# Gated linear attention and a two-level mixture of experts: token pairs of two sequences on the partitions

## The chip, the cores and the metric

One Trainium2 chip, one core. The metric is the device time of the whole kernel in microseconds (us); a run's time is that of the slowest core, and here there is one. TensorE is called PE, its weight loads PEld, VectorE DVE, ScalarE ACT, GpSimd POOL, SyncE SP.

## The reference, cut to what matters

Inputs q, k, v, f_logit have the shape (4 sequences, 8 heads, 768 tokens, 48), in float32.

```
f = sigmoid(f_logit)
for t in range(768):                                   # for each sequence and head
    state = f[t, :, None] * state + outer(k[t], v[t])  # 48 x 48
    y[t]  = q[t] @ state
x = y, heads side by side                              # (3072 tokens, 384)
g = argmax(x @ w_group);  e = argmax(x @ w_expert[g])  # 4 groups of 4 experts
out[token] = softmax weight of g * softmax weight of e * relu(x @ w1[g, e]) @ w2[g, e]
```

The expert matrices are 384 x 1024 and 1024 x 384; each token goes through one of 16 experts.

## The kernel before, in words

**Two stages.** The first computes the attention and the routing, the second sends the tokens of each expert through its two matrices ("passes"). Two early passes, on experts chosen from the first four chunks of tokens, fill PE at the seam of the two stages.

**The attention** is done in chunks of 128 tokens. A unit is one chunk of two sequences with their 8 heads; there are 12 units, two to a chunk (`units`). Tokens lie on the 128 partitions, and for each of the two sequences (index `b`) the free side holds 8 heads of 48 numbers. The work of a unit is cut into steps, each a generator, named by letters in `STAGES`:

- `l` (`load`): four transfers from SP's queue, of f, k, q and v, 384 KB each, in runs of 48 numbers (192 bytes).
- `c` (`bounded`): DVE clamps f from below (L581). `g` (`gated`): ACT makes -log f with Exp and Ln (L591, L594); PE sums it over the tokens up to each token by a product with the triangle `tri` (L600, tile cs, one for each sequence); ACT exponentiates cs with both signs into eq and kh (L601, L602); POOL issues the transfer of the last token's row into `ends` (L607).
- `m` (`multiplied`): DVE makes qh = q*eq and kh = k*min(kh, bound) (L620, L623).
- `t` (`turned`): PE transposes qh and kh, head pairs together (L634), ACT copies them out as Tq and Tk (L635). `b` (`decayed`): the chunk's decay factors, from `ends` (L644, copied out at L645).
- `s` (`scored`): PE multiplies Tk by Tq into the scores ap (L660), in products of 48 x 64 (weights) by 128 columns on quarters of the array; DVE masks them with `tri` into am (L663).
- `n` (`stated`): PE sums kh by v into ds (L677), 16 products with 128 tokens as rows, 64 weight columns, 48 moving columns; DVE adds the old state and multiplies by the decay (L683, L684).
- `w` (`weighed`): PE adds old state by Tq (L698) and v by am (L702, 16 products with 128 rows and 64 weight columns) into y; ACT copies y into xT (L705).
- `d` (`done`): PE makes the logits from xT (lT L718, lg L723), DVE adds them up (L724). `x` (`listed`): PE transposes xT to rows (L743), ACT copies them (L745, L748). `r`: one step of the routing (`route`), which is a chain of some 24 small DVE operations for a chunk, three small groups of PE products (rk L203 and L205, tb L251), and on POOL the issue of a transfer of `meta` (L246).

**The order of the work** on PE, DVE, ACT and SP is written out by hand: the lists `BEGIN` (the first units), `EVEN`, `ODD` and `ORDERS` (the last units) say for each unit i which step of which neighbour comes next (`d-2` is the next step of `d` for unit i-2), and these engines run in that order. POOL's order is chosen by the scheduler when the program is built. An EVEN and an ODD iteration together carry two units and one chunk's routing.

**PSUM** has 8 banks; `bank` hands them out in rotation, so that an allocation waits until the one eight before it has been read.

**The second stage**, 18 passes with the early ones: `up` (hp, L439), `down` (yo, L475 and L460), gathers and scatters of rows by POOL's indirect transfers (L393, L450). The change does not touch it but for the order in which `bank` hands out banks.

Of the kernel before, what the change touches and what calls it, by code (L numbers as in the profile page):

```python
# [18 lines left out]
P = 128  # L19
# [4 lines left out]
def kernel(  # L24
# [42 lines left out]
    ps = ctx.enter_context(tc.tile_pool(name="ps", bufs=8, space=bass.MemoryType.PSUM))  # L67
# [12 lines left out]
    def bank(shape, name):  # L80
        return ps.tile(shape, FP32, tag="bank", name=name)
# [12 lines left out]
    halves = const([P, 2], FP32, "halves")  # L94
    make_upper_triangular(nc, tri, val=1.0, diag=True)
    make_identity(nc, ident)
    nc.vector.memset(onesb, 1.0)
    nc.vector.tensor_tensor(strictb, tri, ident, OP.subtract)

# [419 lines left out]
    with ExitStack() as fast:  # L519
# [7 lines left out]
        for nm, count in (("v", 4), ("eq", 2), ("qh", 3), ("kh", 3)):  # L527
            pads[nm] = [kept([P, 2, H, DP], f"{nm}{i}") for i in range(count)]
        states = [[kept([P, 2, HP, DP], f"st{s}_{i}") for i in range(2)] for s in range(B // 2)]

        def padded():

            for n in range(4):
                for nm in ("eq", "qh", "kh", "v"):
                    if n < len(pads[nm]):
                        nc.vector.memset(pads[nm][n][:, :, :, D:DP], 1.0 if nm == "eq" else 0.0)
                if n == 1:
                    for t in sum(states, []):
                        nc.vector.memset(t[:, :, :, D:DP], 0.0)
                    nc.vector.memset(gw, 0.0)  # L540
                if n < 3:
                    yield
            constants()
            yield
# [9 lines left out]
        def heads(t):  # L554
            return t.rearrange("p b h d -> p (b h) d")

# [5 lines left out]
        SRC = {"f": f_logit, "k": k, "qh": q, "v": v}  # L562

        def parts(i):

            return (slice(0, 1), slice(1, 2)) if i == 0 else (slice(0, 2),)

        def load(i, names):
            c, s = units[i]
            w = live.setdefault(i, {"v": pads["v"][i % 4], "qh": pads["qh"][i % 3]})  # L570
            for nm in names:
                if nm not in w:
                    w[nm] = sb.tile([P, 2, H, D], FP32, tag="ld_" + nm, bufs=3 if nm == "f" else 2, name="ld_" + nm)
                for b in parts(i) if nm == "f" else (slice(0, 2),):
                    nc.sync.dma_start(out=heads(w[nm][:, b])[:, :, 0:D], in_=SRC[nm][2 * s + b.start:2 * s + b.stop, :, c * P:(c + 1) * P, :].rearrange("b h t d -> t (b h) d"))

        def bounded(i):

            for b in parts(i):
                f = heads(live[i]["f"][:, b])  # L580
                nc.vector.tensor_scalar(f, f, -44.0, None, OP.max)  # L581
            yield

        def gated(i):
# [4 lines left out]
            nl = w["f"].rearrange("p b h d -> p b (h d)")  # L589
            for b in parts(i):  # L590
                nc.scalar.activation(nl[:, b], nl[:, b], AF.Exp, bias=0.0, scale=-1.0)  # L591
                if i:
                    yield
                nc.scalar.activation(nl[:, b], nl[:, b], AF.Ln, bias=1.0, scale=1.0)  # L594
            eq, qh, kh = pads["eq"][i % 2], w["qh"], pads["kh"][i % 3]
            w.update(eq=eq, kh=kh)
            yield
            for b in range(2):
                cs = bank([P, H, D], "cs")
                nc.tensor.matmul(cs.rearrange("t h d -> t (h d)"), lhsT=tri, rhs=nl[:, b], start=True, stop=True)  # L600
                nc.scalar.activation(eq[:, b, :, 0:D], cs, AF.Exp, bias=0.0, scale=-1.0)  # L601
                nc.scalar.activation(kh[:, b, :, 0:D], cs, AF.Exp, bias=0.0, scale=1.0)  # L602
                if b:

                    if s == 0:
                        ends[c] = sb.tile([B, H * DP], FP32, tag="ends", bufs=1, name="ends")
                    side(i).dma_start(out=ends[c][2 * s:2 * s + 2, :], in_=eq[P - 1:P].rearrange("o b h d -> o b (h d)"))  # L607
                yield

        def in_order(i, bs):  # L610

            return [(nm, b) for nm in ("q", "k") for b in bs] if i == 0 else [(nm, b) for b in bs for nm in ("q", "k")]

        def multiplied(i):

            w = live[i]
            for nm, b in in_order(i, [slice(0, 1), slice(1, 2)] if i < 2 else [slice(0, 2)]):
                t = heads(w[nm + "h"][:, b])[:, :, 0:D]
                if nm == "q":
                    nc.vector.tensor_tensor(t, t, heads(w["eq"][:, b])[:, :, 0:D], OP.mult)  # L620
                else:

                    nc.vector.scalar_tensor_tensor(out=t, in0=t, scalar=math.exp(SAFE), in1=heads(w["k"][:, b]), op0=OP.min, op1=OP.mult)  # L623
                yield

        def turned(i):
# [4 lines left out]
            for nm, b in in_order(i, range(2)):  # L631
                pt = bank([P, HP, P], "tr_" + nm)
                for a in range(HP):
                    nc.tensor.transpose(out=pt[:, a, :], in_=w[nm + "h"][:, b, 2 * a:2 * a + 2, :].rearrange("t r d -> t (r d)"), identity=ident)  # L634
                nc.scalar.copy(w["T" + nm][:, b], pt)  # L635
                yield

        def decayed(i):

            c, s = units[i]  # L640
            if s:
# [3 lines left out]
                nc.scalar.copy(decays[:, c], gt)  # L645
            yield

        def scored(i):
            w = live[i]
            w["am"] = []  # L650
            for b in range(2):
# [3 lines left out]
                for a in range(HP):  # L655
                    for r in range(2):
                        rows = slice(DP * r, DP * r + D)
                        for u in range(2):
                            half = slice(u * P // 2, (u + 1) * P // 2)
                            nc.tensor.matmul(ap[r][half, a, :], lhsT=w["Tk"][rows, b, a, half], rhs=w["Tq"][rows, b, a, :], start=True, stop=True)  # L660
                yield
                for r in range(2):
                    nc.vector.tensor_tensor(am[:, r], ap[r], tri.unsqueeze(1).broadcast_to((P, HP, P)), OP.mult)  # L663
                yield

        def stated(i):
# [6 lines left out]
            ds = bank([P, 2, HP, D], "ds")  # L673
            for a in range(HP):
                for b in range(2):
                    for r in range(2):
                        nc.tensor.matmul(ds[DP * r:DP * r + DP, b, a, :], lhsT=w["kh"][:, b, 2 * a + r, :], rhs=w["v"][:, b, 2 * a + r, 0:D], start=True, stop=True)  # L677
# [3 lines left out]
            if c:  # L681
                sp = sb.tile([P, 2, HP, D], FP32, tag="sp", bufs=1, name="sp")
                nc.vector.tensor_tensor(sp, old[:, :, :, 0:D], ds, OP.add)  # L683
                nc.vector.tensor_tensor(dst, sp, gv, OP.mult)  # L684
            else:
                nc.vector.tensor_tensor(dst, ds, gv, OP.mult)
            yield

        def weighed(i):
# [3 lines left out]
            ys = [bank([P, HP, P], f"y{b}") for b in range(2)]  # L693
# [6 lines left out]
            for a in range(HP):  # L700
                for b, h in CORNERS:
                    nc.tensor.matmul(ys[b][DP * h:DP * h + DP, a, :], lhsT=w["v"][:, b, 2 * a + (b ^ h), :], rhs=w["am"][b][:, b ^ h, a, :], start=(c == 0 and a == 0), stop=True, skip_group_check=True)  # L702
# [77 lines left out]
        def advance(gens):  # L780
# [9 lines left out]
        BEGIN = """c0 h g0 p g0 g0 m0 m0 m0 m0 l2 t0 t0 t0 t0 c1 g1 g1 s0 s0 s0 s0 g1 g1 p w0 w0 n0 m1 m1 m1 m1 l3 h x0 x0 x0  # L790
            t1 t1 t1 t1 b1 c2 g2 g2 s1 s1 s1 s1 p d0 g2 g2 n0 n1 w1 w1 m2 m2 l4 n1
            d0 x1 x1 t2 t2 t2 t2 c3 g3 g3 x1 s2 s2 s2 s2 w2 g3 g3 d1 w2 n2 m3 m3 c4 g4 g4""".split()
# [273 lines left out]
```

## Time and profile before

| | |
|---|---|
| time, median of 3 runs | 419.07 us (418.96 to 419.28) |
| the profiled execution's own time | 418.5 us |
| its span | 416.7 us, granted clock 1.0 |
| PE, PEld, DVE, ACT, POOL busy | 405.2, 375.7, 267.0, 157.1, 83.2 us |
| DMA packets | 132121, of which 102630 under 512 bytes; 88.98 MB |
| PE's first attention product (cs) | 5.5 us after the span's start |
| the first product of the early passes (hp) | 139.2 us |

Of the 1.8 us between the span and the execution's time the profile shows nothing. A group's line says: line, engine, operation, output tile and inputs, shapes, count; busy time and mean duration in ns; idle time of the engine before it, and what ended that. A matmul in float32 is two records, a transpose one. PE is pipelined: records overlap, so the step from one record's start to the next one's is what a record costs, and its duration is not.

### The profile page before, as it was taken

How to read it: one execution, taken by the hardware profiler on the slowest of the kernel's cores; microseconds unless marked ns; L12 is line 12 of the kernel's file. 1: busy time of each engine (PE TensorE's matmuls, PEld its weight loads, DVE VectorE, ACT ScalarE, POOL GpSimd, SP SyncE). 2: the span in 40 equal slices, each digit the busy share in tenths (PEclk: the TensorE clock that was granted, in tenths of full speed). 3: DMA queues.
4: the chain of work that ended last, by engine and by line, in shares of the span. 5: the costliest groups of instructions: out<-in, count | busy, mean ns of one | idle time of the engine just before them, and what ended most of it. 6: DMA issues, size and time to landing. Idle time of an engine off the chain costs nothing.

```text
span 416.7 us, 10080 instructions
## 1 busy us (share of the span) xinstructions
PE 405.2 (97%) x4055; PEld 375.7 (90%) x4055; DVE 267.0 (64%) x778; ACT 157.1 (38%) x353; POOL 83.2 (20%) x127
## 2 busy tenths in 40 slices
PE   5999999999999999999999999999999999999995
PEld 3888888888788878989999999999999999999992
DVE  5666787878798741540799777495595595594240
ACT  5777766666574411211122131231231231231220
POOL 4000010101012047101041321311322221120230
PEclk9999999999999999999999999999999999999999
DMA  9999897878999639985639477585595695595010
GB/s 172 212 193 213 171 171 139 153 155 154 277 333 389 221 117 354 383 283 224 229 120 320 128 271 232 178 326 174 206 342 143 253 317 195 208 321 163 28 46 25
DMA packets 132121, 88.98 MB, mean 214 GB/s; under 512 B 102630, under 2 KB 122700, under 8 KB 132066
## 3 DMA queue, kind: packets, MB, share of 16 engines
q1 hardware_dynamic: 125666, 75.50, 62.1%
q0 software_dynamic: 5792, 11.92, 9.5%
q10 hardware_dynamic: 608, 0.83, 0.6%
q8 instruction: 34, 0.56, 0.6%
q14 instruction: 21, 0.17, 0.1%
HBM read 78.71 MB, written 9.83 MB: 212 GB/s over the span
## 4 chain that ended last, share of the span: by engine, by line
PE 51%; issue 30%; DMA 7%; POOL 6%; ACT 3%; DVE 2%; POOLq 1%
PE hp L439 12%; PE yo L475 6%; DMA out_dram<-yt,xg 6%; PE y L702 6%; PE ap L660 5%; PE cs L600 4%; PE yo L460 4%; POOL out_dram L450 4%; PE x_ps L743 3%; PE tr_q L634 2%; POOL xg L393 2%; PE tr_k L634 2%; PE ds L677 2%; PE y L698 2%; PE lT L718 2%
## 5 line engine op out<-in xcount | busy, mean ns | idle before, releaser
L439 PE MATMUL hp<-xe,w 128*128 128x128 f32 (+14 forms) x864 | 138.6, 320 | 0.0
L439 PEld LDWEIGHTS hp<-xe,w 128*128 128x128 f32 x864 | 135.8, 190 | 0.8
L475 PE MATMUL yo<-h,w 128*128 128x230 f32 (+13 forms) x672 | 115.8, 333 | 0.0
L422 DVE STREAM_TRANSPOSE yr<-yT 32x192 f32<-32x192 f32 (+1 forms) x208 | 70.5, 339 | 70.5 <-ACT yT L476 67.9
L475 PEld LDWEIGHTS yo<-h,w 128*128 128x128 f32 x672 | 113.7, 190 | 0.2
L415 DVE STREAM_TRANSPOSE xe<-xg 32x192 f32<-32x192 f32 (+1 forms) x208 | 69.7, 335 | 8.6 <-PE hp L439 5.6
L440 ACT ACTIVATE h<-hp 128x256 f32<-128x256 f32 (+14 forms) x72 | 34.4, 478 | 103.5 <-PE hp L439 103.5
L450 POOL DMA_INDIRECT out_dram<-yt,xg x32 | 34.5, 1078 | 150.5 <-ACT yt L447 144.9
L476 ACT COPY yT<-yo 128x230 f32<-128x230 f32 (+13 forms) x42 | 13.5, 326 | 80.5 <-PE yo L475 80.5
L393 POOL DMA_INDIRECT xg<-x_dram,rows_p x30 | 29.7, 990 | 51.3 <-DMA out_dram<-yt,xg 28.7
L663 DVE TENSOR_TENSOR am<-ap,tri 128x512 f32<-128x512 f32 x48 | 29.8, 683 | 13.4 <-PE ap L660 13.4
L702 PE MATMUL y<-am,v 128*64 128x128 f32 x384 | 25.3, 278 | 0.9 <-DVE am L663 0.8
L702 PEld LDWEIGHTS y<-am,v 128*64 128x64 f32 x384 | 20.9, 136 | 5.0 <-issue 2.2
L660 PE MATMUL ap<-Tq,Tk 48*64 48x128 f32 x768 | 23.8, 272 | 0.3 <-ACT Tk L635 0.3
L660 PEld LDWEIGHTS ap<-Tq,Tk 48*64 48x64 f32 x768 | 20.8, 133 | 2.1 <-issue 1.1
L460 PE MATMUL yo<-w,h 128*128 128x384 f32 x64 | 21.3, 486 | 0.0
L600 PE MATMUL cs<-ld_f,tri 128*128 128x384 f32 x48 | 19.7, 536 | 0.4 <-ACT ld_f L594 0.3
L460 PEld LDWEIGHTS yo<-w,h 128*128 128x128 f32 x64 | 11.9, 190 | 7.4
L607 POOL DMA_DIRECT2D ends<-eq x10 | 5.4, 543 | 57.7 <-ACT eq L601 57.7
L447 ACT ACTIVATE yt<-yr,xg 128x384 f32<-128x384 f32 (+13 forms) x26 | 14.4, 605 | 5.4 <-DVE yr L422 5.4
L705 ACT COPY xT<-y 128x512 f32<-128x512 f32 x24 | 12.9, 589 | 8.9 <-PE y L702 8.9
L634 PE MATMUL tr_q<-ident,qh 128*128 128x128 f32 x96 | 15.4, 286 | 0.2 <-DVE qh L620 0.2
(171 smaller groups left out, 367.2 us busy)
## 6 DMA issues: line engine op xcount, KB each, us to landing
w<-in_moe_w_dram SPq DMA_DIRECT2D x34, 1536.0 KB, 10.5
qh<-in_q_dram SPq DMA_DIRECT2D x12, 384.0 KB, 5.0
ld_k<-in_k_dram SPq DMA_DIRECT2D x12, 384.0 KB, 6.1
v<-in_v_dram SPq DMA_DIRECT2D x12, 384.0 KB, 5.8
ld_f<-in_f_logit_dram SPq DMA_DIRECT2D x11, 384.0 KB, 5.7
x_dram<-x_kept SPq DMA_DIRECT2D x2, 1536.0 KB, 11.6
x_dram<-x POOLq DMA_DIRECT2D x2, 384.0 KB, 6.6
x_dram<-x ACTq DMA_DIRECT2D x2, 384.0 KB, 7.9
```

The costliest lines, as they stand in the source:

```text
L393: nc.gpsimd.indirect_dma_start(out=w["x"][:, j, :], out_offset=None, in_=x_dram[0:1 + top, :], in_offset=bass.IndirectOffsetOnAxis(ap=rows ...
L415: squares(w, lambda n, k_, rk, g, rg: nc.vector.transpose(out=xT[rg, 0:n, k_], in_=x[rk, 0:n, g]))
L422: squares(w, lambda n, k_, rk, g, rg: nc.vector.transpose(out=y[rk, 0:n, g], in_=yT[rg, 0:n, k_]))
L439: nc.tensor.matmul(hp[:, o, :], lhsT=w1[:, ko, (f + o) * P:(f + o + 1) * P], rhs=w["xT"][:, ko, :], start=(ko == 0), stop=(ko == KO - 1))
L440: nc.scalar.activation(h[:, f:f + 2, :], hp, AF.Relu)
L450: sent = nc.gpsimd.indirect_dma_start(out=out, out_offset=bass.IndirectOffsetOnAxis(ap=w["x"][0:m, j, DM + 1:RW].bitcast(U32), axis=0), in ...
L460: nc.tensor.matmul(yp, lhsT=w["h"][:, fo, :], rhs=w2[:, fo, :], start=(fo == 0), stop=(fo == FO - 1))
L475: nc.tensor.matmul(yp, lhsT=w2[:, fo, m * P:(m + 1) * P], rhs=w["h"][:, fo, :], start=(fo == 0), stop=(fo == FO - 1))
L600: nc.tensor.matmul(cs.rearrange("t h d -> t (h d)"), lhsT=tri, rhs=nl[:, b], start=True, stop=True)
L634: nc.tensor.transpose(out=pt[:, a, :], in_=w[nm + "h"][:, b, 2 * a:2 * a + 2, :].rearrange("t r d -> t (r d)"), identity=ident)
L660: nc.tensor.matmul(ap[r][half, a, :], lhsT=w["Tk"][rows, b, a, half], rhs=w["Tq"][rows, b, a, :], start=True, stop=True)
L702: nc.tensor.matmul(ys[b][DP * h:DP * h + DP, a, :], lhsT=w["v"][:, b, 2 * a + (b ^ h), :], rhs=w["am"][b][:, b ^ h, a, :], start=(c == 0 a ...
```

## The change

A unit is still one chunk of two sequences, and its 128 partitions now hold 64 pairs of neighbouring tokens of the one sequence and 64 of the other. The free side holds heads, then the two tokens of a pair (index `j`, the parity), then 48 numbers, so that a run of a load is 96 numbers (384 bytes).

- Loads: two transfers for each input, one for each sequence, of 64 partitions. v and q lose their padded tiles for these loads; q is multiplied into qh, which has its own tile.
- `gated`: POOL adds -log f of the two tokens of a pair (tile pair); one PE product with `sums` (a triangle for each sequence) gives the sum up to the second token, cs, for both sequences; DVE subtracts the second token's -log f for the first token (tile first). ACT still makes two eq and two kh, from cs and from first.
- `bounded` runs on POOL from unit 2 on.
- `multiplied`: four DVE operations by parity. `turned`: the copies of Tq interleave the parities back into token order; Tk stays by parity.
- `scored`: by parity of the key instead of by sequence; the products are as large and as many. The mask is `causal`, by parity.
- `stated` and `weighed` (v by am): rows are 64 instead of 128, and the products are twice as many (32 each), on quarters of the array, added up over the two parities. ds takes two banks and its addition is two DVE operations.
- `decayed`: the copy goes from ACT to DVE.
- PSUM: two banks are set aside for y (`held`), six rotate; outside the attention every fourth allocation takes one of the two.
- The lists `BEGIN`, `EVEN`, `ODD` and `ORDERS` are new: in an iteration the state and y products, the scores and the new state's products follow one another, and the four `m` stand two before and two behind the first masks.

```diff
+        held = turns["n"] % 4 == 0
+        return ps.tile(shape, FP32, tag="held" if held else "bank", bufs=2 if held else 6, name=name)
...
-                    nc.sync.dma_start(out=heads(w[nm][:, b])[:, :, 0:D], in_=SRC[nm][2 * s + b.start:2 * s + b.stop, :, c * P:(c + 1) * P, :].rearrange("b h t d -> t (b h) d"))
+                    for b in range(2):
+                        nc.sync.dma_start(out=w[nm][DP * b:DP * b + DP, hs].rearrange("p h j d -> p h (j d)"), in_=SRC[nm][2 * s + b, hs, c * P:(c + 1) * P, :].rearrange("h (p j) d -> p h (j d)", j=2))
...
+                (nc.vector if i < 2 else nc.gpsimd).tensor_scalar(f, f, -44.0, None, OP.max)
...
+                nc.gpsimd.tensor_tensor(pair[:, hs], nl[:, hs, 0], nl[:, hs, 1], OP.add)
...
-            for b in range(2):
-                cs = bank([P, H, D], "cs")
-                nc.tensor.matmul(cs.rearrange("t h d -> t (h d)"), lhsT=tri, rhs=nl[:, b], start=True, stop=True)
...
+            cs = bank([P, H, D], "cs")
+            for hs in parts(i):
+                nc.tensor.matmul(cs[:, hs].rearrange("t h d -> t (h d)"), lhsT=sums, rhs=pair[:, hs].rearrange("t h d -> t (h d)"), start=True, stop=True)
+            first_ = sb.tile([P, H, D], FP32, tag="first", bufs=1, name="first")
+            nc.vector.tensor_tensor(first_, cs, nl[:, :, 1], OP.subtract)
+            nc.scalar.activation(eq[:, 1, :, 0:D], cs, AF.Exp, bias=0.0, scale=-1.0)
+            nc.scalar.activation(kh[:, 1, :, 0:D], cs, AF.Exp, bias=0.0, scale=1.0)
...
+            side(i).dma_start(out=ends[c][2 * s:2 * s + 2, :], in_=eq[DP - 1:P:DP, 1].rearrange("o h d -> o (h d)"))
+            yield
+            nc.scalar.activation(eq[:, 0, :, 0:D], first_, AF.Exp, bias=0.0, scale=-1.0)
+            nc.scalar.activation(kh[:, 0, :, 0:D], first_, AF.Exp, bias=0.0, scale=1.0)
...
+                    nc.scalar.copy(to, pt.rearrange("q a (b t) -> q b a t", b=2))
...
-                nc.scalar.copy(decays[:, c], gt)
+                nc.vector.tensor_copy(decays[:, c], gt)
...
-                        nc.tensor.matmul(ds[DP * r:DP * r + DP, b, a, :], lhsT=w["kh"][:, b, 2 * a + r, :], rhs=w["v"][:, b, 2 * a + r, 0:D], start=True, stop=True)
+            for j in range(2):
+                for a in range(HP):
+                    for b, r in CORNERS:
+                        rows = slice(DP * b, DP * b + DP)
+                        nc.tensor.matmul(ds[b][DP * r:DP * r + DP, a, :], lhsT=w["kh"][rows, j, 2 * a + r, :], rhs=w["v"][rows, 2 * a + r, j, :], start=(j == 0 and a == 0), stop=(j == 1), skip_group_check=True)
...
-                    nc.tensor.matmul(ys[b][DP * h:DP * h + DP, a, :], lhsT=w["v"][:, b, 2 * a + (b ^ h), :], rhs=w["am"][b][:, b ^ h, a, :], start=(c == 0 and a == 0), stop=True, skip_group_check=True)
+                        nc.tensor.matmul(ys[b][DP * h:DP * h + DP, a, :], lhsT=w["vs"][rows, at:at + DP], rhs=w["am"][j][rows, r, a, :], start=(c == 0 and j == 0 and a == 0), stop=(j == 1), skip_group_check=True)
...
-        EVEN = "l+2 d-2 n-1 r r r x-1 x-1 t t t t g+1 g+1 x-1 r s s s s c+2 w d-1 g+2 w g+2 n m+1 m+1".split()
-        ODD = "l+2 d-2 r r x-1 x-1 t t t t b n-1 g+1 g+1 x-1 r s s s s c+2 w d-1 g+2 w g+2 n m+1 m+1 r n".split()
...
+        EVEN = "l+2 n-1 r t t t t g+1 d-2 r x-1 x-1 g+1 x-1 r d-1 w s m+1 m+1 s s n s m+1 m+1 c+2 g+2 g+2 r w".split()
+        ODD = "l+2 b n-1 r t t t t g+1 d-2 r x-1 x-1 g+1 x-1 r d-1 w s m+1 m+1 s s n s m+1 m+1 c+2 g+2 g+2 r w".split()
```

## The prediction

> **What bounds the kernel now.** I read the page's slices first.
>
> ```profile
> PE   5999999999999999999999999999999999999995
> ...
> DMA  9999897878999639985639477585595695595010
> ```
>
> PE is busy from the second slice to the last but one, so a cut elsewhere brings nothing until PE waits. The DMA engines are full only in the first slices, and the loads run ahead of need there: the four inputs of a unit are 1.57 MB, which the 209 GB/s of the third 10 us would bring in 7.5 us, and a unit lasts 10.8. Next, the timeline of PE over one iteration:
>
> ```profile
> 76.28 1.98 PE L660 MATMUL ap<-Tq,Tk 48*64 48x128 f32 x64
> 78.08 1.05 PE L698 MATMUL y<-Tq,st 48*64 48x128 f32 x32
> 79.07 0.64 PE L718 MATMUL lT<-xT,gw 128*32 128x128 f32 x16
> 79.64 2.07 PE L702 MATMUL y<-am,v 128*64 128x128 f32 x32
> 81.54 1.09 PE L677 MATMUL ds<-v,kh 128*64 128x48 f32 x32
> 82.56 0.33 PE L723 MATMUL lg<-ident,lgT 128*128 128x128 f32 x1
> 82.72 1.04 PE L743 MATMUL x_ps<-ident,xT 128*128 128x128 f32 x8
> 83.60 0.60 PE L634 MATMUL tr_q<-ident,qh 128*128 128x128 f32 x4
> ...
> 85.44 0.41 PE L644 MATMUL gt<-ident,ends 4*128 4x4 f32 x4
> 85.78 1.56 PE L600 MATMUL cs<-ld_f,tri 128*128 128x384 f32 x4
> 87.17 0.19 PE L203 MATMUL rk<-ohe,strictb 128*128 128x64 bf16 x1
> 87.20 0.25 PE L205 MATMUL rk<-ohe,onesb 128*128 128x64 bf16 x4
> 87.38 0.34 PE L660 MATMUL ap<-Tq,Tk 48*64 48x128 f32 x4
> ```
>
> Columns: start, length, instruction. Steps between starts are the price, and they follow without a hole: ap 1.80, y of the state 0.99, lT 0.57, y 1.90, ds 1.02, lg 0.16, x_ps 0.88, four tr 1.84, gt 0.34, cs 1.39, rk 0.21, together 11.10. By the chain of waits the neighbour takes 10.57 (ap at 65.79 and 76.36): 21.67 us for a pair of iterations. From 139 to 401 us, the expert passes, PE is busy 261.85 of 262 us; what the attention gains or loses therefore reaches the end whole. DVE comes next:
>
> ```profile
> 73.40 0.16 DVE L220 CAST at<-keys 128x4 int32<-128x4 f32 x1
> ...
> 77.42 2.48 DVE L663 TENSOR_TENSOR am<-ap,tri 128x512 f32<-128x512 f32 x4 [0.38 <-PE ap L660]
> 79.83 0.55 DVE L581 TENSOR_SCALAR ld_f<-ld_f 128x768 f32<-128x768 f32 x1
> 80.29 0.95 DVE L620 TENSOR_TENSOR qh<-qh,eq 128x768 f32<-128x768 f32 x1
> ```
>
> Between 73.40 and 77.42 it had one hole, of 0.38 us: in the iteration with the long routing steps DVE is nearly as full as PE.
>
> **PE's work.** One cs product instead of two: 1.29 us for four records (96.44 to 97.73 in the same timeline), so 0.65 less. That counts for 11 units (the first unit's lies in a chain of latencies): -7.1. y goes from 16 products of 128 rows, two side by side, to 32 of 64 rows, four side by side. The rows of ap and of y of the state show four quarters of 128 columns in 0.109 us, as long as the pairs of y: 16 x 0.109 = 1.75, where 1.90 stood with its slow first records. State, ap, ds and y now follow one another in quarters, which spares changes of shape at 0.1 each (0.99 against 8 x 0.109 = 0.88; 1.02 against 16 x 0.058 = 0.93) and adds one behind y and one ahead of lT at the same price, partly in place of others; I take -0.23 a unit, -2.8 for 12.
>
> ds also goes to 32 products, of 48 columns. Its pairs step by 0.058 us, not by the 0.040 that 48 columns would take at 0.84 ns each, so something other than columns limits it. If quarters start as pairs do, 16 groups x 0.058: no change. If they need what a group of ap needs, 16 x 0.109 = 1.75: +0.82 a unit, +8.2 for 10 units. I take 0, by the nearer row (the same 48 columns), and keep 8.2. [...]
>
> **DVE's work** loses the clamp (0.55) and gains first (0.55, as L683's 548 ns for the same shape), 0.2 by cutting two multiplications in four (541 and 549 ns against half of 950), and gt's copy 0.2 in every second iteration. What matters is the order. In EVEN, from cs to the first masks, DVE has first 0.55, lgs 0.24, the routing steps of 73.40 to 75.55 (2.15), two multiplications 1.09: 4.03. PE has in that time lg 0.16, x_ps 0.88, lT 0.57, state 0.93, half of ap 0.88: 3.42. DVE is 0.6 late. The masks take 2.42 for four; PE has ap 0.88, ds 0.93 and half of y 0.88 = 2.69 before it needs the last: 0.27 is absorbed, some 0.4 reaches PE. Three such iterations (4, 6, 8): +1.2.
>
> **POOL's queue** is the new wait.
>
> ```profile
> 77.48 0.79 POOL L246 DMA_DIRECT2D x_dram<-meta  x1 [10.16 <-DVE table L256]
> L888 POOL MEMSET yT<- 128x384 f32 x2 | 0.8, 443 | 0.0
> ```
>
> Before, POOL sat 10 us in front of the issue of meta and nobody minded. In the built program after, the order in three iterations is clamp, meta's issue, pair: the addition that the next cs needs stands behind a wait for the routing's last DVE step. From ap's first half: masks 2.42, multiplications 1.09, routing 75.55 to 76.92 (1.37), 0.6 late, 0.56 from there to POOL's start, the issue 0.79, pair. PE has in that time 0.88 + 0.93 + 1.75 + 0.4 wait + 0.1, then gt 0.34, tb 0.20, tr 1.75, less 0.16 of latency: 6.2. The pair's price is not in the trace: 0.44 by the memset of the same size (no input), 1.7 by twice three times the 0.28 of a select of 128 columns (one input); I take 0.8, between. 7.6 - 6.2 = 1.4 late, 1.1 to 2.3. What ACT and DVE made ahead gives a little back; I take 1.2 three times, +3.6. [...]
>
> The clamp on POOL (0.7 by three memset steps of 0.24 over a fixed part, 1.2 by the select) runs while DVE does routing and multiplications. Whether the two hinder each other no row shows, since POOL does next to nothing there before: 0 to +1 for each of 9 iterations. I take +1.5 in all. [...]
>
> **Loads and the start.** Runs of 384 bytes halve the packets, of which nobody waits past the start; SP issues twice as many transfers, at 0.53 each where the ring is free (1.06 for two at 0.73 us). For the first unit the first half of f landed 3.24 us after its issue; I take 1 us off, and 0.5 added for pair and first in the chain up to the first ap (11.86): -0.5, from -1.5 to +0.5. ACT loses 0.2 and stays at 70%: nothing. Six rotating banks and two held for y: in ODD two tr wait for ds's readers, some 0.3, inside the wait for pair. In the passes the distance between uses of a bank stays eight: nothing.
>
> **Sum:** -7.1 - 2.8 + 0 + 1.2 + 3.6 + 1.5 - 0.5 = -4.1 against the profiled execution's 418.5: 414.4. The median of the runs stands 0.57 above that execution: 415.0. Changes under 0.2% (0.84 us) a measurement of this kernel can't tell from none.
>
> **Rivals.** *The waits don't come* (0.12): the 4.8 of the two waits and the 1.5 fall away, 408.7. For it: ACT and DVE have slack in every second iteration. Against: the order in POOL's queue is fixed. *DVE held up by POOL, slower* (0.23): the clamp falls in the DVE stretch between cs and the masks, which has no slack: 0.95 less the 0.27 absorbed, 9 times, = +6.1 instead of 1.5: 419.6, and 421.9 with the clamp at 1.2. It turns the sign from 0.62 us an iteration on (5.6 over 9). For it: DVE's single hole. Against: half of the routing's operations are tiny. *Quarters of ds load one after the other, slower* (0.10): +8.2, 423.2. For it: its step above the columns' time; against: ap's quarters start 0.007 us apart. My forecast, 411 to 418, has 0.45; 0.10 is for what I don't see, of either sign.
>
> The range, 408.7 to 423.2, takes in the fast rival and both slow ones, and leaves 2 in 10 outside. Faster: 0.45 and 0.12 and a hundredth of the rest = 0.58; within 0.2%: 0.08, out of the DVE rival's lower end and the forecast's upper; slower: 0.34.
>
> **What would show it.** Right: cs of two records at 0.65 us a unit; y at 1.75; ds near 0.93; ahead of the cs of units 6, 8 and 10 a hole of about 1.2 on PE, released by POOL pair; the first hp near 135 instead of 139.2, and the passes as long as before. Wrong: ds near 1.75; DVE operations of SBUF inputs longer or later beside POOL's clamp; PE waiting for DVE in every iteration; or the passes changed in length, which I priced at nothing.

## The result: 8% slower, and the profile after

The kernel after takes 454.1 us (median of 4 runs, 451.8 to 455.5) where the kernel before takes 419.0 in the same series: a ratio of 1.0837, interval [1.0813, 1.0861]. The profiled execution took 455.5 us, with a span of 453.7. I had predicted 415.0 and a range up to 423.2: both the sign and the size are wrong.

The slices of the page, after:

```profile
PE   2783989888996888999999999999999999999995
PEclk9988889989999799999999999999999999999998
DMA  8998077765757996399838559569658756865210
```

PE is no longer full in the first 16 slices, and the granted clock, a row of full speed before, now has dips. Behind them little is changed. The timeline says it to the tenth: the first hp starts at 174.9 us instead of 139.2, and from there to the end of the span it is 278.8 us instead of 277.5. All but 1.3 of the 37.0 us lost are in the attention. In the rest of this document "first hp" is the yardstick: it is free of what happens in the passes.

The windows up to the first hp, before and after (sums over the stretch, busy time of each engine):

```profile
sum 139.20, PE 132.95 PEld 112.99 DVE 104.74 ACT 93.03 POOL 17.28; mean PE 44.32 PEld 37.66 DVE 34.91 ACT 31.01 POOL 5.76
```

```profile
sum 174.90, PE 138.49 PEld 118.26 DVE 119.35 ACT 93.61 POOL 52.61; mean PE 46.16 PEld 39.42 DVE 39.78 ACT 31.20 POOL 17.54
```

PE's idle time rose from 6.2 to 36.4 us: 30.2 of the 35.7 us lost. PE's busy time should have fallen and rose by 5.5: the record of the granted clock has 23.9 us of this stretch at half speed, in five pieces. Now the waits of PE in that stretch (total, number, longest):

```profile
PE cs L618 <- POOL pair L612: 12.2, 8, 5.6
PE ds L704 <- issue: 4.5, 3, 2.4
PE y L734 <- issue: 3.7, 3, 2.2
PE tr_q L656 <- DVE qh L642: 2.7, 2, 1.8
PE rk L216 <- DVE ohe L211: 2.6, 2, 1.5
...
PE ap L686 <- issue: 1.8, 1, 1.8
```

Added up by what ended them: POOL 12.2 us (before: none), "issue" 11.3 (0.2), DVE 5.8 (1.0), DMA 4.9 (4.0), ACT 1.7 (1.0). "Issue" means that PE waited for nothing the profile shows. One iteration has both kinds (timeline of PE: start, length, instruction, idle time before it and what ended that):

```profile
84.10 0.91 PE L618 MATMUL cs<-pair,sums 128*128 128x384 f32 x2 [0.85 <-POOL pair L612]
84.85 0.27 PE L755 MATMUL lg<-ident,lgT 128*128 128x128 f32 x1
84.96 1.04 PE L775 MATMUL x_ps<-ident,xT 128*128 128x128 f32 x8
85.93 0.65 PE L750 MATMUL lT<-xT,gw 128*32 128x128 f32 x16
86.50 1.10 PE L727 MATMUL y<-Tq,st 48*64 48x128 f32 x32
87.43 1.93 PE L686 MATMUL ap<-Tq,Tk 48*64 48x128 f32 x64
89.17 0.98 PE L704 MATMUL ds<-v,kh 64*64 64x48 f32 x56
92.52 0.34 PE L704 MATMUL ds<-v,kh 64*64 64x48 f32 x8 [2.36 <-issue]
...
93.09 3.43 PE L734 MATMUL y<-am,v 64*64 64x128 f32 x64
```

The hole of 2.36 us lies inside one run of products on inputs that were there all along: 56 records of ds, a gap, the last 8. In that gap the trace has one packet of 16 KB on the queue that carries instructions, from 89.83 to 91.22, and PE goes on 1.30 us after its end. This queue in the window from 89 to 93 us (packets, MB, share of 16 engines' time: 2.2% of 64 us is 1.4 us):

```profile
q8 instruction: 1, 0.02, 2.2%
```

Six more such holes end 1.31 to 1.70 us after a packet's end, and PE has 4737 matmul and 4737 load records where it had 4055 of each (in 39 such packets where there were 34, so some 240 to a packet). Behind the hole y runs at half clock: 3.43 us instead of the 1.85 to 1.91 of undisturbed units.

The largest hole is in the fourth unit (timeline of ACT, POOL and PE):

```profile
39.97 0.91 ACT L608 ACTIVATE ld_f<-ld_f 128x768 f32<-128x768 f32 x1
40.99 2.12 POOL L597 TENSOR_SCALAR ld_f<-ld_f 128x768 f32<-128x768 f32 x1 [6.06 <-ACT ld_f L608]
43.14 0.84 ACT L611 ACTIVATE ld_f<-ld_f 128x768 f32<-128x768 f32 x1 [2.25 <-POOL ld_f L597]
44.06 1.00 POOL L612 TENSOR_TENSOR pair<-ld_f 128x384 f32<-128x384 f32 x1 [0.96 <-ACT ld_f L611]
45.11 1.65 PE L618 MATMUL cs<-pair,sums 128*128 128x384 f32 x2 [5.64 <-POOL pair L612]
```

Exp, clamp, Ln, addition, product: one chain across three engines, entered late because `BEGIN` puts this unit's Exp behind the copies of `x`. The list also has `c3` behind the first `g3`: in this unit the clamp comes after the Exp that it is meant to bound, and stands between it and Ln. Unit for unit, the fourth scores start at 63.6 us instead of 44.1: more than half of the 35.7 us is lost before the steady iterations begin.

POOL's own lines (busy, mean ns), then what DVE does beside them:

```profile
L597 POOL TENSOR_SCALAR ld_f<-ld_f 128x768 f32<-128x768 f32 x10 | 21.4, 2142 | 6.4 <-ACT ld_f L608 6.1
```

```profile
68.77 0.56 DVE L712 TENSOR_TENSOR st<-sp,decays 128x384 f32<-128x384 f32 x1
...
82.48 1.99 DVE L712 TENSOR_TENSOR st<-sp,decays 128x384 f32<-128x384 f32 x1
83.04 1.01 POOL L612 TENSOR_TENSOR pair<-ld_f 128x384 f32<-128x384 f32 x1
86.94 1.08 DVE L208 TENSOR_TENSOR oh<-oh,best 128x80 f32<-128x80 f32 x1
87.08 2.14 POOL L597 TENSOR_SCALAR ld_f<-ld_f 128x768 f32<-128x768 f32 x1
```

The clamp takes 2.14 us, and some DVE operations with two inputs in SBUF that meet POOL are held up: st takes 1.99 instead of 0.56, oh 1.08 instead of 0.24.

### The profile page after: what moved, and what is told of

The parts are those of the page before. It is cut to its first block, busy times and chain, and to the rows that moved or that the text cites. A ratio compares the mean times of both kernels' runs of the same rounds, so it can differ in the third digit from the quotient of the medians.

```text
span 453.7 us, 11611 instructions
## 1 busy us (share of the span) xinstructions
PE 410.8 (91%) x4737; PEld 381.0 (84%) x4737; DVE 282.5 (62%) x819; ACT 157.6 (35%) x347; POOL 119.5 (26%) x151
## 4 chain that ended last, share of the span: by engine, by line
PE 36%; issue 36%; POOL 9%; DMA 9%; DVE 5%; ACT 3%; POOLq 1%; SPq 1%; DVEq 0%
PE hp L452 11%; PE yo L488 6%; DMA out_dram<-yt,xg 6%; PE y L734 4%; PE yo L473 3%; POOL out_dram L463 3%; PE ap L686 3%; POOL xg L406 2%; DMA ld_f<-in_f_logit_dram 2%; POOL ld_f L597 2%; PE y L727 2%; POOL pair L612 1%; PE tr_q L656 1%; PE cs L618 1%; PE ds L704 1%
## 5 line engine op out<-in xcount | busy, mean ns | idle before, releaser
L463 POOL DMA_INDIRECT out_dram<-yt,xg x32 | 34.5, 1079 | 149.9 <-ACT yt L460 144.3
L689 DVE TENSOR_TENSOR am<-ap,causal 128x512 f32<-128x512 f32 x48 | 29.9, 682 | 13.4 <-PE ap L686 13.4
L734 PE MATMUL y<-am,v 64*64 64x128 f32 x768 | 30.7, 296 | 4.4 <-issue 3.7
L734 PEld LDWEIGHTS y<-am,v 64*64 64x64 f32 x768 | 25.5, 148 | 7.8 <-issue 4.8
L686 PE MATMUL ap<-Tq,Tk 48*64 48x128 f32 x768 | 26.0, 287 | 2.5 <-issue 1.8
L686 PEld LDWEIGHTS ap<-Tq,Tk 48*64 48x64 f32 x768 | 23.6, 143 | 3.0 <-issue 2.1
L618 PE MATMUL cs<-pair,sums 128*128 128x384 f32 (+1 forms) x26 | 13.1, 593 | 12.2 <-POOL pair L612 12.2
L597 POOL TENSOR_SCALAR ld_f<-ld_f 128x768 f32<-128x768 f32 x10 | 21.4, 2142 | 6.4 <-ACT ld_f L608 6.1
L620 DVE TENSOR_TENSOR first<-cs,ld_f 128x384 f32<-128x384 f32 x12 | 6.7, 556 | 22.1 <-PE cs L618 11.9
L612 POOL TENSOR_TENSOR pair<-ld_f 128x384 f32<-128x384 f32 (+1 forms) x13 | 12.5, 960 | 27.1 <-ACT ld_f L611 27.0
## 6 DMA issues: line engine op xcount, KB each, us to landing
w<-in_moe_w_dram SPq DMA_DIRECT2D x34, 1536.0 KB, 10.7
x_dram<-x_kept SPq DMA_DIRECT2D x2, 1536.0 KB, 11.9
```

What stands on the lines that cost most here:

```text
L463: sent = nc.gpsimd.indirect_dma_start(out=out, out_offset=bass.IndirectOffsetOnAxis(ap=w["x"][0:m, j, DM + 1:RW].bitcast(U32), axis=0), in ...
L597: (nc.vector if i < 2 else nc.gpsimd).tensor_scalar(f, f, -44.0, None, OP.max)
L686: nc.tensor.matmul(ap[r][half, a, :], lhsT=w["Tk"][rows, j, a, half], rhs=w["Tq"][rows, b, a, :], start=True, stop=True)
L689: nc.vector.tensor_tensor(am[:, r], ap[r], causal[:, j].unsqueeze(1).broadcast_to((P, HP, P)), OP.mult)
L734: nc.tensor.matmul(ys[b][DP * h:DP * h + DP, a, :], lhsT=w["vs"][rows, at:at + DP], rhs=w["am"][j][rows, r, a, :], start=(c == 0 and j == ...
```

## The experiments

Four theories. **Supply**: PE gets its instructions in packets, some 240 products and loads to each, and runs dry where quarters use them up too fast. **POOL**: the clamp and the addition, in the chain to cs, are too slow. **Order**: the new lists put the steps where their inputs aren't ready. **DVE**: its queue, with first and the cut multiplications in it, has become the limit behind the others. The half clock is a follow-up of any of them, since it comes behind holes (in after from 92.7 us on, behind the one of 2.36).

The kernels ran in four rows, each beside the kernel before on the same chip. On the chips of the first and last rows the kernel before itself takes 424.9 us, and in the kernels traced there 283.1 to 284.4 us go by from the first hp to the end, instead of 277.4 to 278.9; so rows are compared by ratios to before and by the first hp.

| kernel | ratio to before, interval | first hp, us | PE's waits up to it: POOL, issue, DVE, us |
|---|---|---|---|
| before | 1 | 139.2 | 0, 0.2, 1.0 |
| after | 1.0837 [1.0813, 1.0861] | 174.9 | 12.2, 11.3, 5.8 |
| split_in_before | 1.0244 [1.0183, 1.0306] | 149.9 | 0, 5.2, 0.2 |
| no_pool | 1.0779 [1.0719, 1.0840] | 166.7 | 0, 7.3, 6.5 |
| ds_wide | 1.0821 [1.0762, 1.0880] | 173.4 | 11.0, 1.6, 7.9 |
| first_later | 1.1046 [1.0959, 1.1133] | 185.1 | 9.4, 8.8, 15.0 |
| after_again | 1.0832 [1.0814, 1.0850] | 169.8 | 9.6, 11.8, 5.6 |
| clamp_dve | 1.0818 [1.0799, 1.0837] | 177.1 | 10.2, 11.2, 8.0 |
| old_order | 1.0536 [1.0519, 1.0554] | 162.1 | 10.1, 2.6, 4.7 |
| old_order_nopool | 1.0479 [1.0449, 1.0509] | 160.1 | 0, 7.0, 4.5 |
| wide_after | 1.0590 [1.0561, 1.0619] | 164.7 | 12.0, 0.8, 9.5 |
| wide_old_nopool | 1.0341 [1.0319, 1.0363] | 152.2 | 0, 0.5, 4.9 |
| old_order_dve | 1.0407 [1.0357, 1.0457] | 155.8 | 3.2, 5.1, 7.5 |
| old_order_alldve | 1.0856 [1.0826, 1.0886] | 178.0 | 0, 3.1, 22.4 |
| wide_old_dve | 1.0294 [1.0250, 1.0337] | 153.2 | 3.1, 1.5, 8.3 |
| no_first | 1.0300 [1.0280, 1.0320] | 151.2 | 4.2, 5.0, 6.1 |
| wide_no_first | 1.0213 [1.0191, 1.0236] | 149.2 | 3.5, 1.4, 7.5 |

The waits are sums of the lines of the view shown above, from one profiled execution each. The two profiles of the kernel after differ by 5.1 us in the first hp, so single profiles tell no less than that.

### Row 1: one part of the change alone, or undone

**split_in_before**: the kernel before, with more instructions. Supply was to bring holes of 1 to 2.5 us that wait for nothing the profile shows, inside y or ap in most iterations, with half clock behind them, and 428 to 445 us.

```diff
-            for a in range(HP):
+            for a, u in HALVES:                     # 64 columns each
+                ts = slice(DP * u, DP * u + DP)
                 for b, h in CORNERS:
-                    nc.tensor.matmul(ys[b][.., a, :], lhsT=.., rhs=w["am"][b][:, b ^ h, a, :], ..)
+                    nc.tensor.matmul(ys[b][.., a, ts], lhsT=.., rhs=w["am"][b][:, b ^ h, a, ts], ..)
```

> The kernel before, with both groups of products of y (L698 and L702) split into products of 64 columns: the same columns and rows as before, but 16 + 16 more products a unit, which is as many instructions more on PE as the change adds with its quarters of y and ds. Nothing else is changed, POOL included. [...] Theory 'POOL' (the 37 us come from cs waiting for POOL): PE has at most the price of the shorter products to pay, 418 to 421, no such holes, clock 1.0.

Measured: 1.0244, 435.4 us where before has 424.9 on this chip, first hp 149.9 instead of 139.2. Holes appear in runs where there were none. PE's timeline, y of the state in the late units:

```profile
114.47 1.11 PE L700 MATMUL y<-Tq,st 48*64 48x64 f32 x63
116.70 0.21 PE L700 MATMUL y<-Tq,st 48*64 48x64 f32 x1 [1.12 <-issue]
```

The packet of instructions came from 114.53 to 115.49, and PE went on 1.21 us behind it. The products themselves got dearer by some 0.2 us a unit (1.04 for 0.98, 1.92 to 2.06 for 1.90), 2 to 2.5 in all; the holes marked issue are 5.2. With no layout, no POOL and no new order, more instructions, dearer products included, slow the kernel by 2.4%. That more instructions bring such holes is shown; that the packets are what PE waits for is read from their times. In size it is the lower end of what I expected: the ratio makes 429 of 419. Some 3 us of the 10.7 up to the first hp are neither holes marked issue nor dearer products; the trace has 1.8 us more of waits for ACT and one stretch of 3.4 us at half clock there.

**no_pool** (clamp on DVE; cs as two accumulated products over `nl[:, :, 0]` and `nl[:, :, 1]`, no addition):

> The kernel after, with the clamp on DVE for every unit, and without the addition of pairs: cs is two accumulated products, one over the even and one over the odd tokens. POOL has no part in the chain to cs any more. Theory 'POOL': the 12.2 us in which cs waits for POOL go, the half clock behind these holes goes too, cs costs 0.65 more in 11 units (+7) and DVE some 2 more: 440 to 448. Theory 'supply': the holes inside ds, y and ap and the half clock behind them stay as they are (some 14 us of holes), 448 to 455, and the first hp is no earlier than 168.

Measured: 1.0779, no different from the kernel after within the intervals, and 452 of 419 by the ratio, as supply has it; the first hp, 166.7, is a little under its 168. The waits for POOL are gone; in their place cs waits 6.4 us for Ln on ACT, whose chain starts as late as before. The issue holes are still 7.3. The theory POOL, as the whole cause, falls.

**ds_wide** (ds in products with the weights of two heads, 128 columns, and 96 moving columns; the diagonal blocks are read):

> The kernel after, with ds made of 16 products a unit of 64 rows x 128 columns of weights x 96 columns (two heads, of which the diagonal blocks are read) instead of 32 quarters of 48 columns: half the instructions of ds on PE, 64 records and 64 weight loads less in each of 10 units. Theory 'supply': the holes inside y and ap shrink by half or more, and with them the stretches at half clock: 437 to 446. Theory 'POOL': only ds itself gets shorter, 16 x 0.081 / 2 = 0.65 instead of 0.93 at best, 10 times: 451 to 454; cs waits for POOL as before (12 us).

Measured: the issue holes fall to 1.6 us, as supply has it, but the time doesn't (453 of 419 by the ratio): ds itself takes 1.96 us a unit instead of 0.98, since its 32 records follow one another at 0.061 us, where after starts four quarters every 0.058. The test doesn't decide; wide_after below does it better.

**first_later**: the subtraction behind the two exponentials that read cs.

```diff
-            nc.vector.tensor_tensor(first_, cs, nl[:, :, 1], OP.subtract)
             nc.scalar.activation(eq[:, 1, :, 0:D], cs, AF.Exp, bias=0.0, scale=-1.0)
             nc.scalar.activation(kh[:, 1, :, 0:D], cs, AF.Exp, bias=0.0, scale=1.0)
+            nc.vector.tensor_tensor(first_, cs, nl[:, :, 1], OP.subtract)
```

> The kernel after, with the subtraction that makes first written behind the two exponentials that read cs (eq and kh of the odd tokens), so that ACT need not wait for DVE before it reads cs. Theory 'order' (eq behind first holds up the multiplications, the transposes and with them PE): the 17.1 us in which ACT waits for first go, eq follows cs within 0.3 us, the first ap starts 0.5 us earlier than 15.46, and the time is 447 to 453. Theories 'supply' and 'POOL': this wait lies beside others, 453 to 456; first may now wait for the exponentials instead, 1.0 us later than before.

Measured: 1.1046 (463 of 419), a good deal slower than the kernel after and over the range of either theory. In the trace of after, ACT waits 17.1 us for first before it reads the same bank of PSUM; turned round, DVE waits for ACT, and longer:

```profile
DVE first L622 <- ACT kh L621: 30.6, 11, 8.7
```

In the built program the second reader waits for the first one, and DVE, which works in the order of the lists, holds the masks behind it (y now waits 7.5 us for am). Which of the two should go first is answered the other way round from what I expected.

### Row 2: the order

**after_again**, the yardstick:

> The kernel after, unchanged, as the yardstick beside the three others of this row of runs and, with some caution, those of the first row: by the spread of its first four runs 450 to 460 where the kernel before has 419 to 425, first hp at 173 to 177, holes of the same three kinds (cs for POOL 12 us, 'issue' 11 us, DVE some 5).

Measured: 453.2 us, as expected but for the first hp, which came at 169.8.

**clamp_dve** (`nc.vector.tensor_scalar(f, f, -44.0, ...)` for every unit):

> The kernel after, with the clamp on DVE for every unit; the addition of pairs stays on POOL. Theory 'POOL': the clamp's 2.1 us is what makes the addition late, so the wait of cs for POOL falls from 12.2 us to under 4, and with it part of the half clock, 8 to 14 less than the kernel after; DVE takes 0.55 more a unit, of which up to 0.5 may reach PE: 3 to 12 less in all. Theory 'order': in the first units the chain Exp, Ln, addition, cs is simply too late in the order of steps, clamp or no clamp; the wait before the cs of the fourth unit stays over 3 us, and the whole gain is under 4.

Measured: 453.5 us, nothing gained. The wait ahead of the fourth cs is still 3.9 us and all waits for POOL 10.2: as the theory order had it, the chain is late with or without the clamp.

**old_order** (the lists of the kernel before, `m+1` four times where it stood twice, the state's `w` ahead of the `s`, and 8 rotating banks):

```diff
-        EVEN = "l+2 n-1 r t t t t g+1 d-2 r x-1 x-1 g+1 x-1 r d-1 w s m+1 m+1 s s n s m+1 m+1 c+2 g+2 g+2 r w".split()
+        EVEN = "l+2 d-2 n-1 r r r x-1 x-1 t t t t g+1 g+1 x-1 r w s s s s c+2 d-1 g+2 w g+2 n m+1 m+1 m+1 m+1".split()
```

> The kernel after with the layout, the clamp and the addition on POOL as they are, but with the order of steps of the kernel before (the four cut multiplications where two stood, the products of the state moved ahead of the scores) and eight rotating banks. Theory 'order': the first four units cost 15 to 20 us less than in the kernel after, since the transposes, cs and the expansions come in the old sequence, and the quarters of y and ds are spread by cs, lg, x_ps and the transposes, so that the holes marked issue fall below 5 us: 15 to 25 less than the kernel after. Theory 'POOL': cs stands even earlier against the addition, so its waits for POOL grow: no more than 5 less, or more than the kernel after. Theory 'supply': as many instructions as in the kernel after, but not in one run: issue holes fall by about half, 5 us.

Measured: 440.8 us, 12.4 less than the kernel after beside it. In the two profiles the fourth scores start at 52.1 instead of 63.1 us and the first hp at 162.1 instead of 169.8: the first units gain 11.0 us, of which 3.3 are lost again behind them, where cs waits 4.3 and 3.0 us for POOL. The issue holes fall to 2.6. The waits for POOL, 9.6 in after_again, stay:

```profile
PE cs L612 <- POOL pair L606: 10.1, 6, 4.3
```

So the order costs 12 us by the medians and 8 by these profiles, less than the 15 to 25 I expected, and what it costs lies in the first units. The lists and the banks went back together; which of the two it was isn't told apart.

**old_order_nopool** (clamp on DVE and two products for cs on top):

> The one before with POOL taken out of the chain as well: the clamp on DVE and cs as two accumulated products over the even and the odd tokens (no addition). What is left of the change is the layout, the quarters of y and ds and first. Theories 'order' and 'POOL' together: the waits of cs go, cs costs 0.65 more in 11 units; 410 to 425 on a chip where the kernel before has 419 to 424. Theory 'supply': the quarters alone keep 5 to 10 us of holes and some half clock: 425 to 437.

Measured: 438.7 us, over the range of either theory. POOL is out, and the issue holes are back at 7.0: what keeps PE from one wait brings it to the next. Its first scores start at 16.4 us instead of 11.9.

### Row 3: the supply by itself

**wide_after** and **wide_old_nopool**: two products of a quarter become one of twice the columns.

```diff
-                for a in range(HP):
+                for a in (0, 2):
                     for b, h in CORNERS:
-                        nc.tensor.matmul(ys[b][.., a, :], lhsT=.., rhs=w["am"][j][rows, r, a, :], ..)
+                        nc.tensor.matmul(ys[b][.., a:a + 2, :], lhsT=.., rhs=w["am"][j][rows, r, a:a + 2, :], ..)
```

> The kernel after, with every two products of y (and of ds) of one quarter made one of twice the columns: 256 instead of 128 (96 instead of 48), with the weights of the first. Half the instructions of y and ds on PE, the same columns, banks, waits and order. Half of the results of these products are not the reference's, so the second stage sorts other tokens; only the stretch up to the first hp is compared. Theory 'supply': the 11 us of holes marked issue go, and part of the half clock: first hp 12 or more before that of the kernel after (169.8 and 174.9 in its two profiles). Theories 'POOL' and 'order': the holes are only a follow-up of the waits for POOL and of the order; first hp comes earlier by no more than the cheaper ds, some 0.2 in each of 10 units: 2 us.

> old_order_nopool with the same products of twice the columns; half of the results of y and ds are again not the reference's, and only the stretch up to the first hp is compared (160.1 there). Theory 'supply': its issue holes, some 9 us by the profile, go: first hp at 148 to 152, and what is left against 139.2 is the late start (4.5) and the waits of the first units. Without 'supply': 158 to 161.

Measured: the issue holes are 0.8 and 0.5 us, from 11.8 and 7.0. First hp 164.7 instead of 169.8 or 174.9, and 152.2 instead of 160.1; by the ratios the whole kernels are 10.1 and 5.8 us faster (0.0242 and 0.0138 x 419), though their second stages sort other tokens. The cheaper ds (0.66 to 0.78 instead of 0.92 to 1.07 in wide_after) is at most 2.8 of it in each. PE's timeline of old_order_nopool, then of wide_old_nopool, the same unit:

```profile
79.25 1.63 PE L726 MATMUL y<-am,v 64*64 64x128 f32 x36
82.13 0.98 PE L726 MATMUL y<-am,v 64*64 64x128 f32 x26 [1.26 <-issue]
```

```profile
75.58 2.07 PE L726 MATMUL y<-am,v 64*64 64x256 f32 x29
```

The same columns in half the instructions run through. wide_old_nopool is where supply had it (148 to 152). In wide_after I expected 12 or more and got 5 to 10: the waits of PE for DVE rose from 5.6 to 9.5, and those for POOL, 12.0, didn't fall.

**old_order_dve** and **old_order_alldve** (old order, clamp on DVE; the addition on POOL, or on DVE with `nc.vector.tensor_tensor(pair[:, hs], ...)`):

> The kernel after in the old order of steps, the clamp on DVE, the addition of pairs on POOL. Theory 'POOL': the clamp of 2.1 us was what made the addition late; without it cs hardly waits any more and keeps its saving of 0.65 in 11 units: 428 to 434 where old_order had 440.8 and old_order_nopool 438.7. Theory 'order and supply': cs still waits some 5 us for the addition and meta, and the issue holes grow as PE comes closer: 435 to 440.

> The same with the addition of pairs on DVE too (0.55 a unit by its twin first): nothing of POOL in the chain, cs at 0.65. If POOL's 1.0 us and the issue of meta ahead of it are what is left, this is 4 to 8 better than old_order_dve, 425 to 432; if DVE's queue is the limit, masks and additions hold each other up and it is as slow as old_order, 438 to 445.

Measured: 1.0407 and 1.0856, 436.5 and 455.8 us: the first as order and supply have it, the second slower than either of its ranges. In the old order the clamp does matter: 1.0536 to 1.0407, 5 us. But moving the 0.55 us of the addition to DVE as well costs 19 us. PE's waits, first of old_order_dve, then of old_order_alldve:

```profile
PE tb L258 <- DVE val L240: 3.5, 4, 1.3
PE cs L612 <- POOL pair L606: 3.2, 4, 1.8
```

```profile
PE tb L258 <- DVE val L240: 11.0, 4, 2.8
PE tr_q L650 <- DVE qh L636: 6.9, 6, 2.2
```

DVE isn't full (busy 119 of 178 us), but it works in the order of the lists: what is put ahead of the routing and the multiplications makes these late, and PE's order waits for them. Of its 178 us 27.3 are at half clock.

### Row 4: what is left

**wide_old_dve**, **no_first** and **wide_no_first** (old_order_dve with the wide products; without first; both):

> old_order_dve with the products of y and ds of twice the columns (half of their results are not the reference's; the stretch up to the first hp is read, 155.8 there). Supply: 7 to 10 us of holes go, some 3 of them because ds gets cheaper: first hp 146 to 149. If DVE's queue is the limit behind it, PE waits for DVE instead and the gain is under 4: 152 to 156.

> old_order_dve without the subtraction first: the exponentials of the even tokens read cs as those of the odd ones do, so q and k of the even tokens get the decay of the pair's second token (not the reference's). DVE has 0.55 a unit less, and ACT no longer waits for DVE ahead of its exponentials. DVE as a limit: the waits of tb for DVE (3.5 us) and part of the waits of tr_q and cs go, first hp 150 to 153. Supply alone: nothing, or more issue holes in place of the waits: 154 to 156.

> Both. If supply and DVE are separate causes, the gains add: first hp 140 to 145, and what remains above 132 (139.2 less the 7 us of PE's saving) is the later start, 3 to 4 us, and POOL's addition. If one hides the other: no better than the better of the two by more than 1 us.

Measured: first hp 153.2, 151.2 and 149.2, from 155.8. These steps are smaller than what single profiles tell; by the ratios, across two chips, the wide products take off 4.7 us, leaving out first 4.5, and both 8.1.

wide_old_dve gained 2.6 up to the first hp where supply by itself was to bring 7 to 10: its issue holes fall from 5.1 to 1.5, but the waits for DVE, ACT and DMA rise by 2.2 together. no_first's first hp lies in the range for DVE, but the wait that this theory named is still there (tb for DVE: 2.9 instead of 3.5), and PE's idle time falls by 1.2 of the 4.6 only. The rest is PE's busy time: the record of its clock begins, at full speed, at 12.7 instead of 22.8 us, and the first scores take 1.98 instead of 3.62 us. The two profiles of the kernel after differ in the same way (14.2 and 19.8 us; 1.98 and 3.62). So leaving out first gains time, but that it does so through DVE's queue isn't shown.

Both together gain 6.6 us, nearly the sum of 7.2, but far from 140 to 145: two separate gains, each smaller than I thought. In wide_no_first, 10.0 us over before, PE is idle for 18.8 us where it was for 6.2; DVE has 7.5 of it, POOL 3.5, issue 1.4.

## Why the prediction was wrong, point by point

**PE's prices were nearly right.** In undisturbed steady units cs takes 0.65 to 0.75 us, y 1.85 to 1.91 (predicted 1.75), ds 0.92 to 1.07 (0.93), the state's part 0.92. The rival of ds in quarters at 1.75 is refuted. The passes kept their length, as said.

**The step that was missing: work was priced in records, and instructions weren't counted.** The prediction doubled the products of y and ds and asked only what their columns cost. Up to the first hp of after, the packets of the instruction queue never come closer together than 3.65 us, start to start, which is some 66 instructions per us at 240 to a packet. ap uses 128 (64 records of products and 64 weight loads) in 1.75 us, y as many, and ds 128 in 0.95, one behind the other: 384 in 4.5 us. Before, ds and y used 64 each, with slower steps between, and PE had 0.2 us of such holes. In after these holes are 11.3 us. The sum had no term for them.

**"+3.6" for the pair in POOL's queue was the right mechanism at the wrong size and in the wrong place**: 12.2 us, of which 1.8 where I put it. The meta wait that I priced at 1.2 three times is there ahead of the cs of units 6, 8 and 10, with 0.85, 0.70 and 0.28 us. The large one, 5.6 us, is in `BEGIN`, which I didn't walk through, and 2.7 are ahead of the very first cs.

**"-0.5" for loads and the start was wrong in sign, and by size the largest miss**: it was the only term for the first units, and the fourth scores come 19.5 us later than before. The first scores start at 15.5 instead of 11.9 us. Line by line, first of before, then three of after:

```profile
4.99 0.36 DVE L581 TENSOR_SCALAR ld_f<-ld_f 128x384 f32<-128x384 f32 x1 [0.64 <-DMA ld_f<-in_f_logit_dram]
```

```profile
6.33 0.47 DVE L597 TENSOR_SCALAR ld_f<-ld_f 128x384 f32<-128x384 f32 x1 [1.53 <-DMA ld_f<-in_f_logit_dram]
8.63 1.01 PE L618 MATMUL cs<-pair,sums 128*128 128x192 f32 x2 [0.99 <-POOL pair L612]
10.33 0.49 ACT L621 ACTIVATE eq<-cs 128x384 f32<-128x384 f32 x1 [2.43 <-DVE first L620]
```

The second half of f is clamped 1.3 us later (the first half 0.45), where I had taken 1 us off for the loads; the chain goes through one more engine, and eq waits for first. Without first the first scores start at 13.9 instead of 15.1 us (no_first and old_order_dve).

**"Clamp 0.7 to 1.2" was 2.14 us**, nearly twice its upper bound: the rows of POOL it was drawn from, memsets and selects, have no such operation among them. The pair, 0.8 from 0.44 to 1.7, measured 1.00.

**The rival "DVE held up by POOL"** has its mechanism: st and oh above, and st on average:

```profile
L712 DVE TENSOR_TENSOR st<-sp,decays 128x384 f32<-128x384 f32 x8 | 8.6, 1080 | 0.3
```

```profile
L710 DVE TENSOR_TENSOR st<-sp,decays 128x384 f32<-128x384 f32 x8 | 4.5, 559 | 0.3
```

(groups of after and of no_pool). But it isn't what set the end: taking the clamp off POOL gained nothing in the new order, nor did taking the addition off as well. st was stretched by 1.43 us beside an addition of 1.01. Beside the clamp of 2.14 oh was stretched by 0.84 us, and the qh behind, also with two inputs in SBUF, took its usual 0.55 while the clamp went on. What decides which operation is stretched, and by how much, isn't shown.

**"DVE late, +1.2"** looked at the masks alone, which PE waits 0.5 us for. DVE shows itself elsewhere, at qh (2.7) and in the routing (rk 2.6, tb), and is the largest wait left when the rest is mended (7.5 us in wide_no_first).

**The account**, as steps of the ratio times 418 us (each kernel by its own before, so the steps cross chips): order and banks 12.4 (1.0832 to 1.0536), clamp off POOL 5.4 (to 1.0407), wide products 4.7 (to 1.0294), of which the cheaper ds is up to 2.8, first 3.4 (to 1.0213). By the first hp of single profiles, from after_again on, the same steps are 7.7, 6.3, 2.6 and 4.0 us, with 10.0 left. About 9 us aren't told apart: the addition on POOL, DVE's longer queue and the later start.

No kernel of these beats the one before.

## What to carry to other kernels

Before products are split, count the instructions per microsecond that the split asks for, not only the columns, and look whether the queue that carries instructions shows packets at their closest spacing (3.65 us in after). An operation that is moved to an idle engine and stands in the chain to the bounding one is priced by its latency, and from a measured row of that operation or not at all. Walk the start-up list step by step like the steady one: half of this loss was there.

## What the runs showed of the hardware that was not expected

- **PE's instruction supply.** Packets of 16 KB, some 240 products and loads each, take 0.88 to 1.39 us in the attention of before and of after, and start no closer than 3.47 us there in before and 3.65 in after, some 69 and 66 instructions per us at most. The seven holes marked issue of 0.3 us or more inside a run of products in after end 1.30 to 1.70 us after a packet's end.
- **The clock falls on little idle time.** The half clock of after comes in three stretches of 3.41 us and two of 6.83 up to the first hp, and every one begins a multiple of 3.41 us behind the record's start at 14.2 us. Windows of after, of the length of such a stretch and ending at such a multiple (PE busy in us, second field; PEclk after POOL):

```profile
24.44:27.86 3.42, 2.08 (x88) 1.85 (x90) 0.33 (x2) 2.83 (x5) 0.47 (x1) 1.00 1.30 223
27.86:31.27 3.41, 3.41 (x72) 3.04 (x67) 2.19 (x5) 0.00 (x0) 0.53 (x1) 0.50 1.30 210
```

```profile
89.30:92.70 3.40, 1.04 (x68) 0.95 (x60) 3.40 (x6) 1.80 (x3) 1.00 (x1) 1.00 0.26 39
92.70:96.10 3.40, 3.40 (x69) 3.31 (x68) 2.01 (x8) 0.00 (x0) 0.00 (x0) 0.50 0.25 63
```

```profile
144.00:147.40 3.40, 1.94 (x37) 1.76 (x37) 3.06 (x13) 0.98 (x3) 0.63 (x2) 1.00 1.16 289
147.40:150.80 3.40, 3.40 (x45) 2.72 (x47) 3.23 (x12) 2.40 (x6) 0.00 (x0) 1.00 1.06 359
150.80:154.20 3.40, 1.59 (x59) 1.35 (x52) 2.62 (x11) 2.50 (x8) 1.21 (x2) 0.99 1.01 339
154.20:161.00 6.80, 6.80 (x113) 6.05 (x112) 4.38 (x11) 0.36 (x1) 1.20 (x2) 0.50 0.85 238
```

  With PE busy 1.04 or 1.59 of 3.4 us the next stretch is at half speed, with 1.94 it isn't, and with 2.08 it is. So there is no sharp bound in these numbers. Ahead of the other two stretches of after, from 41.5 and 58.6 us on, PE is busy 1.37 and 1.27 us; in the windows up to the first hp behind which full speed follows it is busy 1.86 us or more.
- **A clamp of 128 x 768 floats takes 2.14 us on POOL and 0.55 on DVE**; an addition of 128 x 384 takes 1.00 and its twin first 0.55.
